# Scaling the mantissas of a float64 conversion on GpSimd in place of ScalarE

## The chip, the cores and the metric

The kernel runs on one core of a Trainium2 chip. Its time is what the device takes for one launch, in microseconds (us), and less is better. The core has five engines that run side by side, each through its own list of instructions in order: TensorE (PE in the profile; its weight loads are PEld), VectorE (DVE), ScalarE (ACT), GpSimd (POOL) and SyncE (SP), which here only issues DMA transfers. Engines wait for one another through semaphores. A waiting instruction holds up all that stands behind it on its own engine.

## The reference

Attention with a threshold, followed by a Fourier mixing block, for 8 batches of 576 tokens with 8 heads of 64:

```python
scores = scale * np.matmul(q, k.transpose(0, 1, 3, 2))
thresh = np.max(scores, axis=-1, keepdims=True) - tau
scores = np.where(scores >= thresh, scores, -1000000000.0)
...
attn = attn / (np.sum(attn, axis=-1, keepdims=True) + 1e-09)
x = np.matmul(attn, v)      # heads side by side: (8, 576, 512)

mixed = np.real(np.fft.fft(np.fft.fft(x, axis=1), axis=2))
u = x + mixed
un = (u - mu) / np.sqrt(var + 1e-06)
out = u + np.maximum(un @ w_ch1, 0.0) @ w_ch2
```

The two weight matrices are made as float32 arrays times a float64 scalar. They arrive as float64: w_ch1 is 512 x 2048, w_ch2 is 2048 x 512. All other inputs are float32.

## The kernel before

**The two parts.** Attention runs in 160 steps, 20 for each batch: four pairs of heads, five blocks of 128 queries each. A step `i` has the scores (TensorE, L440 and L446, into one of two score buffers per head), the maxima (VectorE, L461), the exponential (ScalarE, L469) and the threshold value (L473), the masked sum (VectorE, L477), the sum's inverse (L385, L388) and its spread copy (ScalarE, L509). In the next step the weights are transposed (TensorE, L587 to L605) and copied out (ScalarE, L593, L607), and products with the values follow (L636), which VectorE or ScalarE takes out (L645). The Fourier mixing of a batch and the two large products with the weights (L909 and L933 for the first group of 512 tokens, L1210 and L1398 for the others, which use a form with fewer multiplications) are cut into pieces and put between the steps of later batches.

**Whose order.** The whole schedule is written out by hand: each engine does its instructions in the order in which the program names them. Nothing is reordered by a tool. Semaphore waits are set for what an instruction reads and writes.

**The conversion.** [...] `convert` gets a chunk as pairs of 32-bit words and does, with a `yield` between stages:

1. the load (SP queue, L286)
2. VectorE: the upper 20 bits of the mantissa into the place of the result (`bits`, L296), and the exponent (`power`, L299)
3. the scaling of these bits to 1 + bits x 2^-20 (L304), and the exponent made that of a float32 (ScalarE, L307)
4. VectorE: the lower word of the mantissa is added (L311)
5. GpSimd: times the power of two (L316)
6. ScalarE: the sign (L318); GpSimd: times the sign (L319)

`dst` and `bits` are the same memory: stage 3 works in place, and L311 reads what it leaves.

**Where the stages stand.** The 16 chunks of w_ch1 go with the steps of the first batch, one a step. In step `i`, `next_stages` runs behind the maxima: stage 2 of chunk `i`, then stages 4 and 5 of chunk `i - 1`. `last_stage`, behind the masked sums, runs stage 6 of chunk `i - 1`. Stage 3 of chunk `i` comes near the end of step `i`, behind the transposed weights (`weights_in_parts`, whose GpSimd copies of v are L576 and L582), behind `prep_ends` (GpSimd, L420), and ahead of the centring of w_ch1 (`less_mean`, L376, on VectorE for two of four rows and on GpSimd for the others) and of the folding of rows for the Fourier mixing (`fold_rows`, L687 to L703, on GpSimd except for a batch's last pair). In step 5 `copy_seq` (L220 to L229) also stands there on GpSimd.

The 16 chunks of w_ch2 go with the steps of the second batch by the table `PLAN`: one or two a step, from its second step to its fifteenth. `second_batch` puts them the same way: `advance(first)` for stage 2, two times `advance(first - 1)` for stages 4 and 5, one more for stage 6, and `advance(first)` near the end of the step for stage 3. Between them the first mixing (`mixing(0)`, whose sums are L803 to L812, some on GpSimd) and the first product (L909) are placed. A chunk's room in `hs` or elsewhere is used for several chunks in turn; a reload (L286) waits until the earlier chunk's stages 4 to 6 are done with it. Loads of q and k (L134) and of v (L149, L152) are in the same SP queue.

**Buffers.** `hs` serves as five staging rooms in the first batch. Score tiles have two buffers, the other PSUM tiles (`mm`) four.

Of the kernel before, what the change touches and what calls it, by code (L numbers as in the profile page):

```python
# [12 lines left out]
ALU = mybir.AluOpType  # L13
ACT = mybir.ActivationFunctionType
# [33 lines left out]
def kernel(  # L48
# [12 lines left out]
    nc = tc.nc  # L61
# [103 lines left out]
    for u in range(2):  # L165
# [14 lines left out]
        out=q_scale[:], in0=tau_t[:], scalar1=0.0, scalar2=SCALE, op0=ALU.is_ge, op1=ALU.mult  # L180
# [3 lines left out]
        out=below[:], in0=tau_t[:], scalar1=0.0, scalar2=-3.0e38, op0=ALU.is_lt, op1=ALU.mult  # L184
# [3 lines left out]
        out=tau_pos[:], in0=tau_t[:], scalar1=0.0, scalar2=-1.0, op0=ALU.max, op1=ALU.mult  # L188
# [90 lines left out]
    def convert(src, dst, raw, power):  # L279

        if src.dtype == FP32:
            nc.sync.dma_start(out=dst, in_=src)
            return
        nc.sync.dma_start(out=raw, in_=src.bitcast(INT32).rearrange("p (c n) -> p c n", c=2))  # L286
        pairs = raw.rearrange("p c (n two) -> p c n two", two=2)
        low, high = pairs[:, :, :, 0], pairs[:, :, :, 1]
        dst = dst.rearrange("p (c n) -> p c n", c=2)
        bits = dst.bitcast(INT32)  # L290
        power = power.rearrange("p (c n) -> p c n", c=2)
        sign = high.bitcast(FP32)

        yield

        nc.vector.tensor_scalar(  # L296
            out=bits, in0=high, scalar1=0xFFFFF, scalar2=None, op0=ALU.bitwise_and
        )
        nc.vector.tensor_scalar(  # L299
            out=power, in0=high, scalar1=20, scalar2=0x7FF,  # L300
            op0=ALU.logical_shift_right, op1=ALU.bitwise_and,
        )
        yield
        nc.scalar.activation(out=dst, in_=bits, func=ACT.Copy, bias=1.0, scale=2.0**-20)  # L304


        nc.scalar.activation(  # L307
            out=power, in_=power, func=ACT.Relu, bias=shift[:, :], scale=float(1 << 23)
        )
        yield  # L310
        nc.vector.scalar_tensor_tensor(  # L311
            out=dst, in0=low.bitcast(UINT32), scalar=2.0**-52, in1=dst,
            op0=ALU.mult, op1=ALU.add,
        )
        yield
        nc.gpsimd.tensor_tensor(out=dst, in0=dst, in1=power.bitcast(FP32), op=ALU.mult)  # L316
        yield
        nc.scalar.activation(out=sign, in_=high, func=ACT.Sign)  # L318
        nc.gpsimd.tensor_tensor(out=dst, in0=dst, in1=sign, op=ALU.mult)  # L319

    def chunk(src, dst, raw, power):
        run = convert(src, dst, raw, power)
        next(run, None)
        return run
# [1583 lines left out]
```

## Time and profile before

| | us |
|---|---|
| median of 3 runs | 1552.85 |
| lowest and highest run | 1552.24, 1553.26 |
| profiled execution | 1552.55 |
| its span, first to last instruction | 1550.8 |

The conversion's groups, as the trace's answers by line have them:

| line | engine | what | times | median ns | first and last start, us |
|---|---|---|---|---|---|
| L296 | VectorE | upper mantissa | 32 | 418 (407 to 971) | 13.2, 236.5 |
| L299 | VectorE | exponent | 32 | 421 (409 to 1517) | 13.5, 236.8 |
| L304 | ScalarE | scaling, int32 to float32 | 32 | 640 | 16.1, 241.2 |
| L307 | ScalarE | power of two | 32 | 719 | 16.6, 241.8 |
| L311 | VectorE | lower mantissa added | 32 | 685 | 18.2, 242.8 |
| L316 | GpSimd | times the power | 32 | 1273 | 19.0, 243.6 |
| L318 | ScalarE | sign | 32 | 687 | 18.6, 243.8 |
| L319 | GpSimd | times the sign | 32 | 1289 | 20.4, 245.0 |

An engine's busy time is the time in which it did an instruction, not the time in which it was needed. Which engine sets the end can differ from stage to stage: so the table of windows gives the busy times for stretches of the span, and the chain of waits follows the work back from the last instruction, at each step to what released it. In rows of an order of time, the first number is the start in us from the span's start and the second the length; a bracket at the end gives the idle time before it and what ended that. "PEclk" is the clock that TensorE was granted, 1.00 being full speed.

### The profile page before, as it was taken

The page shows a single profiled execution, that of the slowest core. Times are in us where ns is not written, and L with a number is a line of the kernel's source. Part 1 is how long each engine was busy: PE and PEld are TensorE (multiplying, and loading weights), DVE is VectorE, ACT ScalarE, POOL GpSimd, SP SyncE. Part 2 cuts the span into 40 slices and gives each one's busy share as a digit, 9 for nine tenths or more (in the row PEclk, how much of TensorE's full clock was granted, in tenths as well). Part 3 has the DMA queues.
Part 4 walks back from the last instruction along what each step waited for, and adds up shares of the span by engine and source line. Part 5 has one row for each costly group of instructions (what it writes and reads, how often), then busy time and mean ns, then how long its engine had stood idle before and what let it go on. Part 6 is the DMA issues. An engine that isn't in the chain of part 4 may idle for free.

```text
span 1550.8 us, 27036 instructions
## 1 busy us (share of the span) xinstructions
PE 1523.1 (98%) x9786; PEld 1185.1 (76%) x9786; DVE 1066.9 (69%) x2141; ACT 917.1 (59%) x1921; POOL 776.8 (50%) x964
## 2 busy tenths in 40 slices
PE   8999999999999999999999999999999999999999
PEld 5555555556788777877788778887788778989999
DVE  7987676846779466866588566956687666746546
ACT  6875675655656576656766666666666676232131
POOL 3775553034365643545254724555264626646635
PEclk9999999999999999999999999999999999999999
DMA  6423233465866344634464354635464534646655
GB/s 168 132 59 119 78 92 108 136 204 159 269 200 189 111 150 133 195 102 141 143 186 140 117 159 135 195 93 166 125 191 135 159 117 140 221 163 226 236 198 184
DMA packets 248907, 239.31 MB, mean 154 GB/s; under 512 B 197027, under 2 KB 218533, under 8 KB 228678
## 3 DMA queue, kind: packets, MB, share of 16 engines
q1 hardware_dynamic: 246262, 237.28, 50.1%
q8 instruction: 78, 1.28, 0.3%
q10 hardware_dynamic: 2512, 0.30, 0.1%
q14 instruction: 55, 0.45, 0.1%
HBM read 205.93 MB, written 31.46 MB: 153 GB/s over the span
## 4 chain that ended last, share of the span: by engine, by line
PE 84%; DVE 9%; ACT 3%; DMA 1%; POOL 1%; issue 1%; SPq 0%; ACTq 0%; DVEq 0%; POOLq 0%
PE ph L1210 25%; PE po L1398 18%; PE sc L440 9%; PE pv L636 9%; PE pw L605 7%; PE po L933 4%; PE ph L909 2%; PE sc L446 2%; PE py L766 2%; PE pa L783 1%; PE pe L587 1%; PE pa L787 1%; PE pm L360 1%; PE po L1377 1%; PE pn L858 1%
## 5 line engine op out<-in xcount | busy, mean ns | idle before, releaser
L520 DVE TENSOR_REDUCE neg<-sc 128x1 f32<-128x576 f32 x216 | 154.2, 750 | 113.0 <-PE sc L440 99.6
L526 ACT ACTIVATE e<-sc,neg 128x576 f32<-128x576 f32 x216 | 158.6, 734 | 121.6 <-DVE neg L520 121.5
L1147 DVE TENSOR_TENSOR hs<-ph,hs 128x512 f32<-128x512 f32 (+1 forms) x128 | 105.4, 823 | 168.0 <-PE ph L1210 97.7
L1398 PE MATMUL po<-w,w_all 128*128 128x128 f32 x1728 | 219.4, 276 | 0.3 <-ACT ends L593 0.3
L1398 PEld LDWEIGHTS po<-w,w_all 128*128 128x128 f32 x1728 | 205.0, 192 | 9.4 <-issue 4.0
L1156 POOL TENSOR_TENSOR w<-hs 128x512 f32<-128x512 f32 x32 | 42.1, 1317 | 313.8 <-ACT hs L1152 240.0
L540 DVE SCALAR_TENSOR_TENSOR e<-sc,thr,e 128x576 f32<-128x576 f32 x216 | 168.3, 812 | 20.6 <-ACT thr L530 20.6
L1210 PE MATMUL ph<-u_t,w 128*128 128x256 f32 x768 | 180.9, 382 | 0.5 <-DMA w<-f 0.5
L440 PE MATMUL sc<-kT,qT 64*128 64x288 f32 x1024 | 169.8, 431 | 7.1 <-DVE e L477 6.1
L607 ACT COPY e_t<-pw 128x512 f32<-128x512 f32 x256 | 148.6, 595 | 44.1 <-PE pw L605 42.7
L605 PE MATMUL pw<-ident,e 128*128 128x128 f32 x1152 | 168.8, 273 | 6.0 <-ACT ends L593 1.9
L549 ACT ACTIVATE e<-e,den 128x576 f32<-128x576 f32 x216 | 157.4, 775 | 8.9 <-DVE den L388 8.2
L1210 PEld LDWEIGHTS ph<-u_t,w 128*128 128x128 f32 x768 | 140.9, 190 | 23.6 <-issue 5.3
L1210 PE MATMUL ph<-w_all,w 128*128 128x256 f32 x672 | 157.1, 382 | 1.1 <-DVE w_all L1132 1.0
L605 PEld LDWEIGHTS pw<-ident,e 128*128 128x128 f32 x1152 | 134.8, 141 | 21.9 <-issue 5.6
L1152 ACT ACTIVATE hs<-hs 128x512 f32<-128x512 f32 (+1 forms) x96 | 74.1, 772 | 114.5 <-DVE hs L1147 113.7
L1210 PEld LDWEIGHTS ph<-w_all,w 128*128 128x128 f32 x672 | 123.4, 190 | 23.9 <-issue 4.9
L440 PEld LDWEIGHTS sc<-kT,qT 64*128 64x128 f32 x1024 | 96.3, 187 | 57.1 <-issue 23.7
L1263 POOL TENSOR_TENSOR w_all<-w_all 128x128 f32<-128x128 f32 (+2 forms) x160 | 118.4, 757 | 29.1 <-DVE w_all L1418 20.2
L1398 PE MATMUL po<-w,hs 128*128 128x128 f32 x912 | 120.0, 278 | 0.3 <-ACT ends L593 0.3
L1398 PEld LDWEIGHTS po<-w,hs 128*128 128x128 f32 x912 | 109.9, 192 | 9.9 <-issue 8.0
L593 ACT COPY ends<-pe 128x128 f32<-128x128 f32 (+1 forms) x128 | 38.1, 298 | 58.7 <-PE pe L587 40.1
(227 smaller groups left out, 2945.3 us busy)
## 6 DMA issues: line engine op xcount, KB each, us to landing
w<-f SPq DMA_DIRECT2D x150, 1024.0 KB, 4.9
hs<-in_moe_w_ch_dram SPq DMA_DIRECT2D x23, 512.0 KB, 4.7
q_in<-in_q_dram SPq DMA_DIRECT2D x128, 72.0 KB, 4.3
out_dram<-u SPq DMA_DIRECT2D x36, 256.0 KB, 2.5
k_in<-in_k_dram SPq DMA_DIRECT2D x124, 72.0 KB, 2.4
v_in<-in_v_dram SPq DMA_DIRECT2D x64, 128.0 KB, 5.0
f<-w SPq DMA_DIRECT2D x14, 512.0 KB, 3.3
f<-w SPq DMA_DIRECT2D x7, 1024.0 KB, 4.8
```

Source lines behind the costliest of these rows:

```text
L440: nc.tensor.matmul(sc[j][:, c, 0:HALF], qT[hp, 128 * t : 128 * t + 128], kT[hp, k0 + HALF * c : k0 + HALF * (c + 1)], start=True, stop=True,)
L520: nc.vector.tensor_reduce(out=neg[:, j : j + 1], in_=sc[j][:, :, 0:HALF], axis=AXIS_XY, op=ALU.max, negate=True,)
L526: nc.scalar.activation(out=ej, in_=sc[j][:, :, 0:HALF], func=ACT.Exp, bias=neg[:, j : j + 1], scale=1.0)
L540: nc.vector.scalar_tensor_tensor(out=ej, in0=sc[j][:, :, 0:HALF], scalar=thr[:, j : j + 1], in1=ej, op0=ALU.is_ge, op1=ALU.mult, accum_out ...
L549: nc.scalar.activation(out=e[:, S * j : S * (j + 1)], in_=e[:, S * j : S * (j + 1)], func=ACT.Copy, scale=den[:, j : j + 1],)
L605: nc.tensor.transpose(pw[:, c, :], e[:, c0 : c0 + 128], ident[:, :])
L607: nc.scalar.copy(e_t[:, 4 * j : 4 * j + 4, qs], pw[:, :, :])
L636: nc.tensor.matmul(pv[64 * j : 64 * j + 64, 0:m], vt[:, 2 * c + j, :], e_t[:, 4 * j + c, 0:m] if c < 4 else ends[:, 0, 0:m], start=(c == 0 ...
L1147: nc.vector.tensor_tensor(out=to, in0=bank, in1=to if other is None else other, op=ALU.add)
L1210: nc.tensor.matmul(bank[:, 256 * q : 256 * q + 256].rearrange("p (two n) -> p two n", two=2), left[:, 256 * c + 128 * q : 256 * c + 128 * ...
L1263: return lambda: eng.tensor_tensor(out=to, in0=to, in1=other, op=ALU.add)
L1398: nc.tensor.matmul(to, lefts[m][j][:, s], right_[:, 128 * s : 128 * (s + 1)], start=jn in (0, 4) and s == 0, stop=s == 3, skip_group_check ...
```

## The change

In stage 3 of `convert` the first of two ScalarE instructions becomes a GpSimd instruction with the same input and output and the same arithmetic. It stands at the same place in the program, and so in GpSimd's list it follows what GpSimd was given before it, in place of ScalarE's list. The lines of the file keep their numbers up to L303; the new call begins at L304.

```diff
         yield
-        nc.scalar.activation(out=dst, in_=bits, func=ACT.Copy, bias=1.0, scale=2.0**-20)
-
-
+        nc.gpsimd.tensor_scalar(
+            out=dst, in0=bits, scalar1=2.0**-20, scalar2=1.0, op0=ALU.mult, op1=ALU.add
+        )
         nc.scalar.activation(
             out=power, in_=power, func=ACT.Relu, bias=shift[:, :], scale=float(1 << 23)
         )
```

L307 and all that follows it keep their line numbers.

## The prediction

> **What bounds the kernel now.** I began with the page's busy shares, then read the window table by stage (first and last us of the window, its length, then busy time of PE, PEld, DVE, ACT, POOL).
>
> ```profile
> span 1550.8 us, 27036 instructions
> ...
> PE 1523.1 (98%) x9786; PEld 1185.1 (76%) x9786; DVE 1066.9 (69%) x2141; ACT 917.1 (59%) x1921; POOL 776.8 (50%) x964
> ```
>
> ```profile
> 40.00:80.00 40.00, 38.34 (x202) 22.87 (x202) 36.22 (x82) 32.62 (x71) 30.68 (x43) 1.00 0.43 123
> ...
> 320.00:360.00 40.00, 40.00 (x190) 22.32 (x189) 20.69 (x45) 19.28 (x38) 21.84 (x31) 1.00 0.64 191
> ```
>
> TensorE (PE) is busy 98% of the span, and wholly so after 262 us. Whatever is lost or won before that moves the end by as much. The 32 conversions, and so the change, lie between 13 and 246 us. There VectorE (DVE) is at 36.2 of 40 us, ScalarE (ACT) at 32.6, GpSimd (POOL) at 30.7: POOL, at half of the span, is not idle where it gets the new work.
>
> Next the chain of waits, for ScalarE's scalings (L304) on it. Start and length:
>
> ```profile
> 78.39 0.47 ACT w L304
> ...
> 172.47 0.53 ACT w_all L304
> 173.00 0.61 ACT u_t L307
> 173.61 0.52 ACT w_all L304
> ```
>
> L304 stands there seven times: at 78.39, 172.47, 173.61, 197.84, 198.98, 219.92 and 221.06, some 3.7 us in all. The other 25 are hidden behind VectorE and TensorE. Last, the order of time on POOL and on VectorE:
>
> ```profile
> 42.70 0.35 POOL L220 MEMSET seq_xe<- 128x290 f32 x1
> ...
> 46.76 1.27 POOL L316 TENSOR_TENSOR w<-w,hs 128x512 f32<-128x512 f32 x1
> ...
> 50.93 0.70 POOL L582 COPY v_rev<-v_in 128x630 f32<-128x630 f32 x1
> 51.60 1.28 POOL L316 TENSOR_TENSOR w<-w,hs 128x512 f32<-128x512 f32 x1
> ```
>
> ```profile
> 50.20 0.72 DVE L311 SCALAR_TENSOR_TENSOR w<-hs,w 128x512 f32<-128x512 uint32 x1
> ...
> 67.15 1.52 DVE L299 TENSOR_SCALAR hs<-hs 128x512 int32<-128x512 int32 x1
> ```
>
> From 42.70 to 51.60 POOL has no gap. VectorE's L311, the first reader of a scaled chunk, starts at 50.20, before POOL's queue has come to the place where the scaling will stand.
>
> **Price of the new instruction.** The trace shows no such instruction on POOL: int32 in, fp32 out, a multiply and an add, 128x512. Its bounds are one-input copies from below and two-input products from above:
>
> ```profile
> L319 POOL TENSOR_TENSOR w<-w,hs 128x512 f32<-128x512 f32 x16 | 20.6, 1290 | 1.2
> ...
> L630 POOL COPY x<-x_first 128x256 f32<-128x256 f32 x2 | 0.8, 398 | 0.0
> ...
> L674 POOL COPY x<-x_first 128x576 f32<-128x576 f32 x1 | 0.7, 657 | 0.0
> ```
>
> The copies give 0.81 ns for an element and so 0.6 us for 512; the product took 1.29 us. It reads one tensor, as a copy does, so I take S = 0.7 us, a tenth over the copy for the conversion and the second operation, and keep 0.6 and 1.3 as ends. The Trainium skill, "GPSIMD Engine Reference", section 3.1, gives 769 ns for a tight one-input loop over 512 elements; by that figure my sum would be about 0.7 us higher.
>
> **What goes.** ScalarE loses 32 x 0.64 = 20.5 us, nearly all behind other work. On the chain: at 78.39 the queue behind L304 ends in the L593 for which TensorE stood idle 1.92 us until 81.85: 0.5 won. At 172.47 and 173.61 VectorE idled 3.34 us until the copy L864: 1.05 won. At 219.92 and 221.06 TensorE waited 0.72 us for L607, so 0.7 is all that can be won. At 197.84 and 198.98 nothing: the chain goes on through the loads of q and k (L134), which also had to wait for VectorE's transpose L411, done at 199.86 against 200.12. Gains: 2.3 us. I count no other.
>
> **What comes.** POOL gets 32 x 0.7 = 22 us. No DMA moves to another queue. L311's wait is now for POOL. Behind L311 on VectorE stand both L477, the sums L385 and L388, L645 and the transposes; TensorE's next scores wait for L477 (two score buffers), ScalarE for L645, the load queue for L411. So a late L311 delays the whole loop wherever VectorE is on the chain. In POOL's queue the scaling of chunk i stands behind L319 of chunk i-1 and behind that step's copies (L420, L576, L582), and its reader L311 comes one step later. I went through all chunks; where POOL is free well before L311 (at 166.3, where L311 follows at 169.52, say) the cost is nothing, and its idle time covers it. The others, at S = 0.7 and, in brackets, at 1.3:
>
> Step 2: POOL is free at 23.03, L311 starts at 23.56. L299 stands between and would be held up too: S - 0.2 = 0.5 (1.1).
>
> Step 7: chunk 5's scaling pushes the gapless run by S, chunk 6's adds another. It ends at 51.60 + 2S, 2.8 (4.0) after 50.20. Of this 0.29 was a wait of L477 for ScalarE and 0.85 is TensorE's own work (L605 ends at 52.88, L477's first half at 52.03). Left: 1.65 (2.85).
>
> Ports: L299 at 67.15 took 1.52 us against its median of 0.42, while POOL ran L376:
>
> ```profile
> 66.83 1.56 POOL L376 TENSOR_TENSOR w<-w,mean 128x512 f32<-128x512 f32 x1
> ```
>
> L376 ends at 68.39 and L299 at 68.67, so the one waited for the other. The Trainium skill, "SBUF — State Buffer", section "Who interferes with whom", says of this: VectorE's second port pair is GpSimd's only one, and whichever comes first holds it for a whole instruction. That speaks against this change, which takes the work from ScalarE, whose ports are its own. Without the rule and the row the sum would be the second rival's.
>
> Where the new instruction pushes POOL's next work under VectorE's L296, L299 and L311, these wait. Step 8: L687 comes about 1.2 us later against VectorE than before: 1.0 (1.4). Step 10: the scaling and L376 share the time around L299: half of S, 0.35 (0.65). Step 11: L376 ended at 73.29 and held up L296 (0.63 us); now S later: 0.7 (1.3). Step 15: two scalings are ahead of the L376 at 97.12, which then covers L296 at 98.62: 1.2 (2.2). All four are on the chain.
>
> Mixing, 139.8 to 153.6: POOL is on the chain without a gap.
>
> ```profile
> 152.76 0.83 POOL u_t L812
> 153.59 0.04 issue
> 153.64 5.42 PE ph L909 x12
> ```
>
> One scaling falls into it, behind L376 at 145.1: S = 0.7 (1.3). The next stands behind the L812 shown; the L311 it delays has its cover in TensorE's L909 until 159 us.
>
> Second batch: chunk 6's scaling would come at 187.7, behind L582, with L311 at 188.27; held up with L299, 0.45 (1.2). Chunk 7's stands behind the folds that end at 194.46, L311 at 194.66: 0.5 (1.1). VectorE is busy from there to L411 and the load that it waits for at 209.69, so both stay. Chunk 11's two end at 222.5, and the L477 that they delay has TensorE's L636 for cover. POOL's L319, for which reloads (L286) wait, gets later too; the two loads for which VectorE waited stood behind other loads, not behind POOL: nothing.
>
> The sum: 0.5 + 1.65 + 1.0 + 0.35 + 0.7 + 1.2 + 0.7 + 0.95 = 7.05, less 2.3 = 4.75 us slower (3.7 at S = 0.6; 13.1 - 2.3 = 10.8 at 1.3). The profiled execution took 1552.55 us, 0.3 under the median of the runs, with 1.75 outside the span. 1552.55 + 4.75 + 0.3 = 1557.6 us.
>
> A term of unknown sign is the clock. After the idle 1.92 us before 81.85 the granted clock was 0.50 to 0.69 until 86 us; an idle time of 1.18 us at 181 left it at 1.00. Step 7's new idle time of 1.65 lies between, and the old one shrinks. L440 and L636 took 2.23 and 2.69 there against 1.91 and 2.31: 0.7 us either way. I take zero.
>
> **Rivals.** First, POOL is dear: S near a product's 1.3. For it speaks that integer input and two operations are more than any copy here does; against it, one tensor read. 1552.85 + 10.8 = 1563.6. GpSimd is then the bound of the first batch.
>
> Second, the port waits go away or VectorE slips in between POOL's instructions, and only waits for the value itself stay: 0.2 + 1.65 + 0.7 + 0.65 = 3.2, less 2.3: 1553.8, no change that can be told. For it: L692's small pieces let VectorE's instructions through (L296 0.55 at 92.26). Against it: the row at 67.15.
>
> Third, faster: ScalarE was the hidden bound. All seven L304 leave the chain (3.7) and with the shorter idle time before 81.85 the clock stays up (0.7), while the late L311 are hidden behind TensorE's queue up to some 1.0 us, in step 7: 1552.85 - 3.4 = 1549.4. It decides where POOL's waits come to under 1.3 us in all; step 7 alone holds it back, since POOL is 1.4 us late there at price zero.
>
> That the change is not reached is excluded: L304 stands 32 times in the trace.
>
> **Chances.** Within 0.2% (3.1 us) a measurement can't tell a change of this kernel. Forecast, 1556 to 1560: 0.46. POOL dear: 0.22. No port waits: 0.22. Faster: 0.08. The 0.02 left goes to slower. So slower 0.70, same 0.22, faster 0.08. The range, 1553 to 1564, takes in the forecast, the second rival and most of the first.
>
> **What would show it.** The new POOL row of 128x512 from int32: 0.6 to 0.8 us, 32 times. L311 of step 7 two to three microseconds later, released by POOL. L296, L299 and L311 longer on average. ScalarE about 20 us less busy; TensorE alike after 262 us. The prediction is wrong if the price is over 1 us, if L311 hardly waits, or if the first 250 us get shorter.

## The result, and the profile after

| | before | after |
|---|---|---|
| median of 18 runs each, same chip, us | 1551.70 | 1556.36 |
| lowest and highest, us | 1549.84, 1555.58 | 1554.23, 1558.97 |
| ratio, 95% interval | | 1.0029 [1.0022, 1.0037] |
| profiled execution, us | 1552.55 | 1558.29 |

The change makes the kernel 4.7 us slower, against 4.75 forecast. Agreement this close is luck: a second comparison of the same two kernels gave 3.9 us, and the runs at equal clock 5.2 (both below). The profiled execution of after is one of the slower runs, 1.9 us above its median.

The page of after, its span and busy shares:

```profile
span 1556.5 us, 27031 instructions
...
PE 1526.1 (98%) x9786; PEld 1187.4 (76%) x9786; DVE 1072.3 (69%) x2141; ACT 903.1 (58%) x1889; POOL 799.7 (51%) x996
```

GpSimd has 32 instructions and 22.9 us more, ScalarE 32 fewer and only 14.0 us less. VectorE does the same 2141 instructions in 5.4 us more: nothing was added to it, so its instructions got longer.

The answer of after for L304, now on GpSimd (lowest, median and longest ns, then first and last start), with who waited for it (us in total, times):

```profile
L304 POOL TENSOR_SCALAR w<-w x16: 620/620/722, 13.4 to 106.4; 128x512 f32<-128x512 int32 x16
L304 POOL TENSOR_SCALAR w_all<-w_all x16: 620/622/1127, 151.5 to 247.2; 128x512 f32<-128x512 int32 x16
...
  DVE w_all L311: 2.6, 4
  DVE w L311: 1.7, 1
```

The price of the new instruction is 0.62 us, near the copies and not near the product: the first rival (GpSimd dear at 1.3) is out. Only five of the 32 readers waited for it by these rows.

Step 7 in the order of time, GpSimd of after (start, length):

```profile
51.55 0.71 POOL L582 COPY v_rev<-v_in 128x630 f32<-128x630 f32 x1
52.34 0.62 POOL L304 TENSOR_SCALAR w<-w 128x512 f32<-128x512 int32 x1
...
57.25 1.73 POOL L687 TENSOR_TENSOR half<-x 128x287 f32<-128x287 f32 x2
```

and VectorE of after:

```profile
49.57 1.30 DVE L296 TENSOR_SCALAR w<-hs 128x512 int32<-128x512 int32 x1
...
52.99 0.69 DVE L311 SCALAR_TENSOR_TENSOR w<-hs,w 128x512 f32<-128x512 uint32 x1 [1.75 <-POOL w L304]
...
57.39 0.94 DVE L296 TENSOR_SCALAR w<-hs 128x512 int32<-128x512 int32 x1
58.25 1.01 DVE L299 TENSOR_SCALAR hs<-hs 128x512 int32<-128x512 int32 x1
```

Both kinds of cost are here. L311 started at 50.20 before; now it stands until 52.99, released by the scaling that had to queue behind the copies of v. In step 8 nothing waits for a value: L296 and L299, which have a median of 0.42, take 0.94 and 1.01 while the two L687 run on GpSimd.

The same shift shows in every step that the prediction named. The table takes the start of each step's maxima (L461) and how much later it is than before's, from one profile of each kernel. The right column is a second profile of the same changed kernel, taken in an experiment below.

| start of step | before, us | after, later by | changed kernel again, later by |
|---|---|---|---|
| 0 | 11.87 | -0.36 | -0.88 |
| 3 | 26.30 | +0.05 | -0.46 |
| 7 | 48.10 | +0.13 | -0.39 |
| 8 | 54.09 | +1.72 | +1.19 |
| 9 | 62.08 | +2.82 | +2.22 |
| 12 | 77.38 | +3.48 | +2.71 |
| 13 | 84.91 | +2.46 | +1.69 |
| 15 | 97.28 | +2.08 | +1.31 |
| 16 | 102.94 | +3.76 | +2.79 |
| 17 | 108.08 | +6.32 | +2.80 |
| 22 | 142.06 | +6.32 | +2.79 |
| 25 | 166.84 | +7.16 | +3.64 |
| 26 | 177.24 | +6.10 | +2.58 |
| 30 | 204.04 | +7.62 | +4.86 |
| 33 | 229.63 | +6.16 | +2.87 |

From step 33 to the last step both columns move by less than 0.7 us (they end at +5.59 and +2.20): nearly all of the change happens in the first two batches. Up to step 16 the two columns run side by side, 0.5 us apart from the start on and 1.0 in the end. Then after loses 2.5 us in one step that the other does not lose, although both have the same program. That is the clock. TensorE of after around it:

```profile
104.41 2.99 PE L440 MATMUL sc<-kT,qT 64*128 64x288 f32 x8 [2.51 <-DVE e L477]
```

and its windows there (length, busy time of PE, PEld, DVE, ACT and POOL, granted clock, DMA):

```profile
104.00:106.00 2.00, 1.59 (x6) 1.47 (x7) 1.93 (x8) 0.50 (x2) 1.92 (x2) 0.50 0.00 0
106.00:108.00 2.00, 2.00 (x9) 0.80 (x8) 1.88 (x3) 0.96 (x2) 0.93 (x2) 0.50 0.02 4
```

The changed kernel again, same place, TensorE and window:

```profile
103.65 1.94 PE L440 MATMUL sc<-kT,qT 64*128 64x288 f32 x8 [2.51 <-DVE e L477]
```

```profile
104.00:106.00 2.00, 2.00 (x12) 1.31 (x12) 1.93 (x7) 1.02 (x2) 1.85 (x3) 1.00 0.02 4
```

The idle time ahead of the scores is the same 2.51 us. In one execution the clock fell to 0.50 behind it and the eight matmuls took 2.99 us; in the other it stayed at 1.00 and they took 1.94. So a single profile can't tell what the change costs; the runs must be sorted by their clock.

### The profile page after: what moved, and what is told of

Its sections match the earlier page's. It is cut to its first block, busy times and chain, and to the rows that moved or that the text cites. A ratio compares the mean times of both kernels' runs of the same rounds, so it can differ in the third digit from the quotient of the medians.

```text
span 1556.5 us, 27031 instructions
## 1 busy us (share of the span) xinstructions
PE 1526.1 (98%) x9786; PEld 1187.4 (76%) x9786; DVE 1072.3 (69%) x2141; ACT 903.1 (58%) x1889; POOL 799.7 (51%) x996
## 4 chain that ended last, share of the span: by engine, by line
PE 85%; DVE 8%; ACT 2%; POOL 2%; DMA 1%; issue 1%; POOLq 0%; ACTq 0%; DVEq 0%
PE ph L1210 25%; PE po L1398 18%; PE pv L636 9%; PE sc L440 9%; PE pw L605 7%; PE po L933 4%; PE ph L909 3%; PE sc L446 2%; PE py L766 2%; PE pe L587 1%; PE pa L783 1%; PE pa L787 1%; PE po L1377 1%; PE pn L858 1%; DVE w_all L1191 1%; DVE neg L520 1%
## 5 line engine op out<-in xcount | busy, mean ns | idle before, releaser
L440 PEld LDWEIGHTS sc<-kT,qT 64*128 64x128 f32 x1024 | 97.5, 187 | 60.6 <-issue 26.6
```

The source lines that it names most:

```text
L440: nc.tensor.matmul(sc[j][:, c, 0:HALF], qT[hp, 128 * t : 128 * t + 128], kT[hp, k0 + HALF * c : k0 + HALF * (c + 1)], start=True, stop=True,)
```

## The experiments

In all but the repeat of the change, a set of chunks says which scalings GpSimd gets; the others stay on ScalarE. A pair (1, n) is chunk n of the first matrix, (2, j) chunk j of the second (their order in the second batch falls from 15 to 0).

```diff
+        if key in on_pool:
+            nc.gpsimd.tensor_scalar(
+                out=dst, in0=bits, scalar1=2.0**-20, scalar2=1.0, op0=ALU.mult, op1=ALU.add
+            )
+        else:
+            nc.scalar.activation(out=dst, in_=bits, func=ACT.Copy, bias=1.0, scale=2.0**-20)
```

The lines of these kernels are shifted by 2 to 12; the tiles have the same names.

### One matrix alone

```diff
+    on_pool = {(1, n) for n in range(16)}
```

> Only the 16 chunks of the first batch are scaled on GpSimd; those of the second batch stay on ScalarE. My theory (VectorE waits in steps 2, 7, 8, 10, 11 and 15, by the value or by the ports): the first-batch terms stay, 0.5 + 1.65 + 1.0 + 0.35 + 0.7 + 1.2 less 0.5 = 4.9 us, and the clock's loss on top where TensorE idles long enough; so 4 to 6.5 us slower than before, ratio 1.0026 to 1.0042. Rival (the loss comes from the mixing and the second batch, where GpSimd is on the chain): 0 to 1 us, ratio under 1.0007.

Measured: 1556.64 against 1550.51, ratio 1.0035 [1.0022, 1.0048]. By the medians the first matrix alone costs as much as the whole change, as expected.

```diff
+    on_pool = {(2, j) for j in range(16)}
```

> Only the 16 chunks of the second batch are scaled on GpSimd. My theory: 0.7 us lost in the mixing and 0.95 behind the folds against 1.75 won on ScalarE, so -1.5 to +0.5 us, ratio 0.9990 to 1.0003. Rival (mixing and second batch make the loss): 3 us or more, ratio over 1.002.

Measured: 1551.27 against 1550.51, ratio 1.0005 [0.9996, 1.0013]: nothing that can be told; the ratio lies a little above the expected range, but its interval reaches into it. In its trace the second batch shows the forecast's terms, each larger, against one another: 0.85 later over the mixing, 1.07 won back in second-batch step 5, 1.3 lost up to step 10, 1.5 won at step 11 to 12.

This run shows something else, since its first batch is that of before, instruction by instruction. It has the same 1.92 us of idle TensorE ahead of 81.87. Its window behind that:

```profile
82.00:84.00 2.00, 2.00 (x16) 1.29 (x18) 1.78 (x5) 1.74 (x5) 2.00 (x3) 1.00 0.51 117
```

and before's:

```profile
82.00:84.00 2.00, 2.00 (x10) 1.42 (x11) 1.48 (x4) 1.59 (x4) 2.00 (x3) 0.55 0.63 144
```

With the clock at 1.00 the maxima of step 16 came 1.57 us earlier than before's, from equal starts at step 12. So the profile on which the prediction was made had lost 1.6 us there to the clock.

### The change again

> The change as it is, on one chip with the three kernels beside it, to part the runs by their mean granted clock. Theory: at a mean clock of 1.000 it stays 4 to 5.5 us over the kernel before at 1.000 (the sum of my terms without the clock is 4.75), and its other runs lie lower in clock than those of before. Rival (the clock makes most of the loss): at 1.000 less than 2 us apart.

Measured: 1554.76 against 1550.89, ratio 1.0025 [1.0015, 1.0036], the changed kernel without an edit. Four of its seven runs had a mean clock of 1.000; with four of the 18 first ones, there are eight such runs, between 1554.23 and 1554.77, median 1554.6. The kernel before has twelve such runs in the three comparisons of the experiments, 1548.76 to 1550.40, median 1549.4. At equal, full clock the change costs 5.2 us. What the clock takes on top is 1.8 for after (1556.4 - 1554.6) and some 1.5 for before (1550.9 - 1549.4), so it hides in the comparison of medians. One part of the expectation missed: the change's other runs were not lower in clock (the mean over all runs was 0.9990 against 0.9985 for before).

### The chain alone

The one chunk whose L304 stood ahead of the idle time of 1.92 us:

```diff
+    on_pool = {(1, 11)}
```

> Of all 32 chunks only chunk 11 of the first batch is scaled on GpSimd; it shortens TensorE's idle time of 1.92 us in step 12, behind which the granted clock fell in the trace of before. Theory (the clock falls behind a long enough idle time): 0.5 us from ScalarE and 1 to 1.6 us from the clock, so 1.5 to 2.1 us faster, ratio 0.9986 to 0.9991, and nearly all runs at a mean clock of 1.000. Rival (the clock falls by chance, not by this idle time): 0.5 us, ratio 0.9995 to 1.0000, and a spread of clocks as before.

Measured: 1548.35 against 1550.99, ratio 0.9983 [0.9974, 0.9992], faster. Ten of its eleven runs had a clock of 1.000, of the kernel before three of 19. Its TensorE after the step and one window:

```profile
80.42 0.66 PE L610 MATMUL pw<-ident,e 128*128 128x128 f32 x4 [1.40 <-ACT ends L598]
```

```profile
82.00:84.00 2.00, 2.00 (x21) 1.25 (x20) 1.94 (x5) 2.00 (x4) 1.46 (x2) 1.00 0.57 112
```

The idle time is 0.52 shorter, which is the step's own gain (the two maxima are 5.80 us apart against 6.32 in the run of the second matrix alone, both at full clock), and the clock stays. How much of the 2.6 us is the clock's follows from the runs at full clock: there the two kernels are 1.1 us apart (1549.4 - 1548.3), so the clock has some 1.5. With the only three full-clock runs of before in this comparison (median 1550.3) it has only some 0.6. What goes beyond 0.52 at full clock is not this step's: in the trace, step 10 of the second batch, where nothing was changed, is 0.59 shorter than before's. VectorE waits there for a chunk's load, and that load's time varies (see "Second batch" below).

Then that chunk and the four of the second batch which stood on the chain with a gain:

```diff
+    on_pool = {(1, 11), (2, 11), (2, 10), (2, 3), (2, 2)}
```

> Only the five chunks whose ScalarE scaling stood on the chain of waits and cost the most are scaled on GpSimd: chunk 11 of the first batch and the pairs of steps 5 and 11 of the second. Theory: the gains of 0.5, 1.05 and 0.7 to 1.05 us without the losses: 2 to 3 us faster than before, ratio 0.9980 to 0.9988. Rival (ScalarE's time is hidden everywhere, the chain misleads): ratio 0.9995 to 1.0005.

Measured: 1546.52 against 1550.89, ratio 0.9970 [0.9959, 0.9981]; all six runs at a clock of 1.000. It is faster than both kernels, and by more than I expected: 4.4 us, of which 2.9 remain at equal clock (1549.4 - 1546.5), against 2.25 by the prediction's gains (0.5 + 1.05 + 0.7). In its trace step 12 is 0.52 shorter than in the run of the second matrix alone, and the second batch's steps 5 and 12 are each 1.04 shorter than before's; step 12 is the one that the prediction capped at 0.7. Its chain through step 12:

```profile
77.22 0.19 ACT rec L514
77.41 0.47 ACT hs L312
...
77.91 0.75 ACT e L474
```

L312 is the power of two (L307 before): the exponential follows it straight away, and the scaling that stood between them before is gone.

The two chunks of which the prediction said that their L304 is on the chain but gates nothing:

```diff
-    on_pool = {(1, 11), (2, 11), (2, 10), (2, 3), (2, 2)}
+    on_pool = {(1, 11), (2, 11), (2, 10), (2, 7), (2, 6), (2, 3), (2, 2)}
```

> The five chunks of the run e6_chain_only and the pair of step 8 of the second batch, whose ScalarE scalings also stood on the chain, ahead of the loads of q and k. Theory (VectorE's transpose is the true gate of these loads, 0.26 us before ScalarE was done): 0 to 0.3 us less than e6_chain_only, ratio 0.9965 to 0.9975. Rival (ScalarE is the gate): 1 us less, ratio 0.9960 to 0.9967.

Measured: 1546.76 against 1550.99, ratio 0.9972 [0.9962, 0.9981], the same as without them. To be on the chain is not to be worth something: the first load of q in step 8 was issued 8.23 us after the start of the step's maxima, against 8.22 in the run of five chunks and 8.23 in before.

### Load without a reader

The scaling stays on ScalarE, and GpSimd does an instruction of the same form on a tile of its own that nothing reads:

```diff
+    on_pool = set()
...
+        nc.gpsimd.tensor_scalar(
+            out=t1_room[...], in0=t1_room[...].bitcast(INT32),
+            scalar1=2.0**-20, scalar2=1.0, op0=ALU.mult, op1=ALU.add,
+        )
```

> ScalarE scales as before; at the place of the change GpSimd does one more instruction of the same shape on memory of its own, for which nobody waits (and one memset at the start). The output is the reference's. Theory: GpSimd's time and the ports cost by themselves: steps 8, 10, 11, 15 and the mixing, 1.0 + 0.35 + 0.7 + 1.2 + 0.7 = 4 us, without the gains of ScalarE; 3 to 6 us slower, ratio 1.002 to 1.004, with longer L296, L299 and L311 in the trace. Rival (it is the wait for the value that costs, not the load): only the mixing's 0.7, ratio under 1.0010.

Measured: 1556.40 against 1550.51, ratio 1.0037 [1.0024, 1.0049]. Its answers: GpSimd's groups by shape between 10 and 130 us (busy us and mean ns of one, idle time before), then VectorE and GpSimd in the order of time.

```profile
L314 POOL TENSOR_SCALAR t_room<-t_room 128x512 f32<-128x512 int32 x15 | 9.5, 635 | 1.2
```

```profile
68.26 1.75 DVE L323 SCALAR_TENSOR_TENSOR w<-hs,w 128x512 f32<-128x512 uint32 x1
```

```profile
68.14 1.32 POOL L388 TENSOR_TENSOR w<-w,mean 128x512 f32<-128x512 f32 x1
```

L323 is L311 and L388 is L376: here the reader takes 1.75 us in place of 0.69 while GpSimd's L376 runs, although it waits for no value from GpSimd. Step 7 costs only 0.29 in this trace, against 1.58 in the changed kernel. So two costs are apart: the value that comes late costs step 7, and the occupied queue and ports cost the rest. What isn't there either is the gain, since ScalarE keeps its work. The prediction's costs without the waits for the value (step 7 and chunks 6 and 7) come to 7.05 - 1.65 - 0.95 = 4.45; measured 5.9. The clock has a part in that: this profile has two falls (from 84.6 and from 105.0 us, 3.4 us each), before's one, and none of its five runs was at 1.000.

The change and that load together:

```diff
+    on_pool = {(1, n) for n in range(16)} | {(2, j) for j in range(16)}
...
+        nc.gpsimd.tensor_scalar(
+            out=t1_room[...], in0=t1_room[...].bitcast(INT32),
...
```

> The change, and behind each scaling GpSimd does one more instruction of the same shape on memory of its own (and one memset at the start): what it would be if the scaling cost twice the 0.62 us seen. The output is the reference's. Theory: my sum at a price of 1.3 us, 10.8 us slower than before and some clock on top: 9 to 14 us, ratio 1.006 to 1.009. Rival (beyond one instruction GpSimd's idle time covers the rest): ratio 1.003 to 1.004.

Measured: 1560.95 against 1550.99, ratio 1.0063 [1.0049, 1.0077]. Another 0.62 us for each chunk costs another 5.3 us by the medians (10.0 - 4.7), and 4.2 at full clock by its one run there (1558.83 - 1554.6). The prediction's two sums, 4.75 at S = 0.7 and 10.8 at 1.3, are somewhat steeper: 10.1 us for each us of price, against 5.3 / 0.62 = 8.5 or 4.2 / 0.62 = 6.8.

### Undoing single costs

Without the two chunks that made GpSimd late in step 7:

```diff
+    on_pool = ({(1, n) for n in range(16)} | {(2, j) for j in range(16)}) - {(1, 5), (1, 6)}
```

> As the change, but chunks 5 and 6 of the first batch are scaled on ScalarE. Theory: VectorE's wait in step 7 goes (1.65 us), the clock's loss behind it too (about 1.4 us in the trace of the changed kernel), and part of step 8: 1 to 3 us slower than before, ratio 1.0005 to 1.002. Rival (step 7 is hidden or paid elsewhere): as the change, 1.0029.

Measured: 1556.64 against 1550.51, ratio 1.0034 [1.0023, 1.0045]. This missed: I expected a good part of step 7's 1.65 back. In the trace it is back. VectorE:

```profile
51.57 0.72 DVE L316 SCALAR_TENSOR_TENSOR w<-hs,w 128x512 f32<-128x512 uint32 x1
```

The reader (L316 here) has no wait, and step 7 takes 0.09 less than before's. But the medians don't show the time saved: step 15 costs 2.1 in place of 1.48, and none of the seven runs had a clock of 1.000 (mean 0.9973; low from 17 to 21 and from 102.4 to 109 us in the profile, where the scores took 3.00 us). At the start of step 15 this profile is 2.0 us ahead of the changed kernel again (0.15 later than before against 2.19, each counted from its own start); steps 15 and 16, which the second low stretch covers, then take 4.60 more than before's in place of 1.48. How much of the loss is the clock's and how much is work that now collides elsewhere stays open.

Without the four chunks whose scalings push GpSimd's next work under VectorE's instructions:

```diff
+    on_pool = ({(1, n) for n in range(16)} | {(2, j) for j in range(16)}) - {(1, n) for n in (7, 9, 10, 14)}
```

> As the change, but chunks 7, 9, 10 and 14 of the first batch, whose scaling on GpSimd pushes its other work under VectorE's L296, L299 and L311, are scaled on ScalarE. Theory: the terms of steps 8, 10, 11 and 15 go in good part: 2 to 4 us less than the change, ratio to before 1.0000 to 1.0016. Rival (port waits are small, waiting for the value makes the loss): ratio as the change, 1.0025 or more.

Measured: 1554.10 against 1550.89, ratio 1.0019 [1.0011, 1.0028], between what the two theories gave. Step 8 costs 0.42 in place of 1.03, steps 10 and 11 nothing in place of 0.49; step 15 still costs 1.2, with one scaling ahead of L376 in place of two and with the clock falling at 101.5 us. So the waits at the ports are real in steps 8, 10 and 11; in step 15 this run doesn't separate ports and clock.

The scaling placed earlier in GpSimd's list, ahead of the copies of v, behind the multiplication of the chunk before:

```diff
+        yield
...
             stages(2)
+            if i in chunks:
+                next(chunks[i])
...
             advance(first - 1)
+            advance(first)
```

> As the change, but the scaling of chunk i is put right behind L316 of chunk i - 1 in GpSimd's list, ahead of L319 and of that step's copies, so that its reader one step later finds it done. GpSimd has the same work. Theory: the waits for the value in steps 2 and 7 and behind the folds of the second batch go (0.4 + 1.6 + 0.6 us), the port terms stay: 1 to 3 us slower than before, ratio 1.0007 to 1.0020. Rival (GpSimd's load alone sets the loss, wherever the scaling stands): ratio 1.0025 or more.

Measured: 1554.52 against 1550.89, ratio 1.0022 [1.0014, 1.0031], in between again. Its VectorE in steps 7 and 8:

```profile
49.12 1.78 DVE L317 SCALAR_TENSOR_TENSOR w<-hs,w 128x512 f32<-128x512 uint32 x1
...
54.43 1.34 DVE L298 TENSOR_SCALAR w<-hs 128x512 int32<-128x512 int32 x1
```

The wait for the value is gone (step 2 is 0.45 shorter than before's, and step 7 costs 0.2 in place of 1.58), but the instructions are held up by GpSimd's next ones instead, and step 8 costs 1.88. In this place the wait that was moved became a wait beside GpSimd's work; whether another place avoids it was not tried.

## Why the prediction was right, point by point

The kernel got slower by the waits on GpSimd in the first two batches, as forecast, and by about the forecast amount. Set side by side at full clock (the changed kernel's second profile; from step 12 to 16 against the run of the second matrix alone, whose first batch is before's at full clock):

| term | predicted | measured |
|---|---|---|
| price S of one scaling | 0.7 (0.6 to 1.3) | 0.62 |
| step 2, behind L299 | 0.5 | 0.42 |
| step 7, value late | 1.65 | 1.58 |
| step 8, L687 under L296 and L299 | 1.0 | 1.03 |
| steps 10 and 11, L376 | 0.35 + 0.7 | 0.49 |
| step 12, gain at 78.39 | -0.5 | +0.17 |
| step 15, L376 | 1.2 | 1.46 |
| mixing | 0.7 | 0.85 |
| second batch, step 5 | -1.05 | -1.06 |
| second batch, chunks 6 and 7 | 0.95 | 2.28 |
| second batch, steps 10 to 12 | -0.7 | -1.99 |
| sum | 4.75 | 5.2 |

The gains on record were rounded up by 0.05. The runs at full clock say 5.2 as well (1554.6 - 1549.4). That the sum comes within 0.5 is in part luck: steps 10 to 12 and 15 are off by 0.3 to 0.7 and the two last terms by 1.3 each, and these errors nearly cancel.

**Price.** Right: the copies were the right neighbours (0.6 to 0.7), and the figure of 769 ns that the Trainium skill gives for a tight loop over 512 elements ("GPSIMD Engine Reference", section 3.1) is too high for this instruction by a quarter: measured 620.

**Waits for the value.** Right in place and size in step 7. In step 2 the size was right, but 0.41 of its 0.42 comes with the load without a reader too, so it is not the value that costs there. The mixing, on after's chain:

```profile
148.95 2.47 POOL w L376 x2
...
151.49 0.80 POOL w_all L304
...
159.91 0.83 POOL u_t L812
```

A scaling stands in the gapless run of GpSimd that ends in TensorE's product, as foreseen.

**Ports.** The second rival (these waits go away) is out. VectorE's L296, L299 and L311 come to 54.7 us in all in before's trace, 54.8 with the second matrix alone, 60.0 in after and 60.6 with the load without a reader; and without their chunks steps 8, 10 and 11 lose their cost or most of it. So GpSimd's work lengthens VectorE's, with no value passed between them, and it does so in the first batch alone. That what they share is a port is the rule that the prediction named; no run here separates it from another shared part. Steps 10 and 11 were put at 1.05 and cost 0.49. The instruction that was held up was another one than I named: in step 11 of after L376 starts at 76.26, so L296 gets through and L311 is held up in its place.

```profile
76.22 0.44 DVE L296 TENSOR_SCALAR w<-hs 128x512 int32<-128x512 int32 x1
...
76.91 1.77 DVE L311 SCALAR_TENSOR_TENSOR w<-hs,w 128x512 f32<-128x512 uint32 x1
```

**The gains.** In the run of chunk 11 alone the 0.5 at 78.39 is there to the digit (0.52). In the whole change it is not, since step 12 gets costs that I had not counted: L296 takes 0.69 in place of 0.42, and L477 still waits 0.19 for the threshold. In the run without chunks 7, 9, 10 and 14 the 0.52 is there again, so what takes it away is those chunks' work on GpSimd. With 0.17 measured in place of -0.5 this is the largest miss of a term in the first batch.

**Second batch.** The two terms for chunks 6 and 7 and for the steps after them are mis-sized by 1.3 each, in opposite directions; that their sum is right (0.25 predicted, 0.29 measured) is luck. The cap of 0.7 was wrong, as the 1.04 of the five chunks' run shows. The rest is a term that the prediction put at nothing: the loads of two chunks for which VectorE waits, in steps 7 and 10. Step 10 in before, and in the run of the first matrix alone, whose second batch has no edit (L298 is L296):

```profile
209.69 0.43 DVE L296 TENSOR_SCALAR w_all<-hs 128x512 int32<-128x512 int32 x1 [4.23 <-DMA hs<-in_moe_w_ch_dram]
```

```profile
211.28 0.43 DVE L298 TENSOR_SCALAR w_all<-hs 128x512 int32<-128x512 int32 x1 [3.12 <-DMA hs<-in_moe_w_ch_dram]
```

The load had been issued 5.57 us earlier in the first and 4.46 in the second, and step 10 of the second is 0.73 shorter, the same as in the changed kernel's second profile. So some 0.7 of the -1.99 is not the change's. In step 7 of that profile the load was issued 2.28 us after the start of the maxima, in before 0.34; what held it up there stays open, and with it how much of the 2.28 is the change's.

**The clock.** The step that failed in its reason is "I take zero", with 0.7 either way, a size read from two rows of matmuls. The clock was worth 1.6 us in the very profile that I argued from, and 2.5 us in one step of after's. The net was near zero only because both kernels lose about as much by it on average. The third rival (faster, since the shorter idle time keeps the clock up) has its mechanism right, as the run of chunk 11 shows, and its price wrong: the late values and the ports in the other steps cost more than it brings.

**Signs.** Of the four that I named, L311 of step 7 came 2.8 us later, released by GpSimd; L296, L299 and L311 got longer; the price was in its bounds; and behind step 33 little moves. TensorE is not wholly busy after 262 us, as the prediction has it from one window: in before's trace it idles 13.7 us there. ScalarE got 14 us less busy and not 20. The lengths of its instructions, summed over the traces, fell by 21.6 us (1056.5 to 1034.9), 20.4 of them L304's; the busy time counts stretches in which two records overlap once, and so fell by less.

## What to carry to other kernels

Moving work to an engine with idle time is decided instruction by instruction: at each, ask whether the old engine's instruction gates the chain and whether the new engine's queue and ports are free there. Here the same edit, at 32 places, cost 0.3%, at the five places where it takes something off the chain and collides with nothing, it won 0.3%. A term that comes and goes from run to run, like the clock here, is to be sized from its own window before it is set to zero.

## What the runs showed of the hardware

**The clock falls by windows of 3.41 us.** In the thirteen profiles the granted clock fell to 0.5 eleven times in the first two batches. Summed from the windows' clock, each fall lasted 3.40 to 3.42 us or just twice that (6.83 in after, in the run without chunks 5 and 6 and in the run without 7, 9, 10 and 14). Where one profile has two falls, their starts are whole windows of 3.413 us apart: 56.2 and 104.0 in after (14.0 windows), 84.6 and 105.0 with the load without a reader (6.0), 17.1 and 102.4 without chunks 5 and 6 (25.0). So the clock is set at the edges of windows that stand still within an execution and lie elsewhere in the next one. Laid out from each fall, the window just ahead of it held this much idle time of TensorE: 1.91, 1.92, 1.93, 2.10, 2.17, 2.21 and 2.22 us in seven of the eleven. No other complete window of the first two batches, in any of the thirteen profiles (in five of them with edges laid back from a fall at the end), held more than 1.86. That explains how the same idle time of 1.92 us had both outcomes: in before it lay in one window, from 78.8 to 82.2, and in the run of the second matrix alone the edge at 81.0 cut it into 1.07 and 0.85. The 2.51 us ahead of step 16's scores in the changed kernel's two profiles differ in the same way. After's window, and that of the second profile, whose edges are laid back from its one fall, at its end (1553.46 us):

```profile
100.59:104.00 3.41, 1.32 (x8) 0.72 (x6) 3.41 (x5) 2.70 (x7) 2.27 (x3) 1.00 0.00 0
```

```profile
99.38:102.79 3.41, 1.75 (x9) 0.91 (x7) 3.41 (x5) 3.13 (x8) 2.35 (x3) 1.00 0.00 0
```

TensorE was busy for 1.32 and 1.75 us of them: 2.1 idle, and the clock fell, against 1.66, and it stayed. It also explains why 1.40 us, left by the scaling of chunk 11 on GpSimd, is safe: it can't fill 1.9 us of a window. Four falls stay open: the windows ahead of them held 1.05, 1.16 and 1.23 us, and the one at 17 us 1.08.

The Trainium skill, "TensorE: Matmul & The Clock Gate", section "Part 1: The HAM clock gate", has the window (4096 cycles, some 3.4 us), that it runs freely, and the half clock; these runs agree in all three. It gives an idle window as what it takes to fall; here a little over half a window of idle time was enough. Within one kernel, 0.001 of mean clock is about 0.9 us (after: 1554.5 at 1.000, 1558.5 at 0.995 and 0.996).

**An instruction that nobody reads.** A 0.62 us GpSimd instruction, once for each of 32 chunks and without a reader, cost 5.9 us (1.0037), the clock's part included: neither its engine (51% busy) nor a data dependency explains it without VectorE's instructions, which got longer where GpSimd ran (0.69 to 1.75).
